# Linear attention and two mixing layers on one core: the decay table made by scans, first loads in halves, last product in two pieces

## The chip, the cores and the metric

The kernel runs on one core of one Trainium2 chip. Its engines are TensorE (matmuls, written PE in the profile; its weight loads are PEld), VectorE (DVE), ScalarE (ACT), GpSimd (POOL) and SyncE (SP), which issues most DMA transfers. Each engine works off its own list of instructions in order and waits on semaphores for the others. The metric is the device time of one execution in microseconds (us), the median of some runs.

## The reference

Three stages, batch 2, 768 tokens, 512 features. First an attention with a decaying state in 8 heads of 64 features:

```python
gamma = 1.0 - 2.0 ** (-5.0 - np.arange(H))
scale = 1.0 / np.sqrt(D)
for t in range(S):
    state = gamma[None, :, None, None] * state + np.einsum('bhd,bhe->bhde', k[:, :, t], v[:, :, t])
    y[:, :, t] = scale * np.einsum('bhd,bhde->bhe', q[:, :, t], state)
```

Then a token mixing of rank 32 and a layer of width 2048:

```python
u = x + ((x^T @ U) @ V)^T
x = u + np.maximum(u @ w_ch1, 0.0) @ w_ch2
```

And a gated layer with a spatial product:

```python
h = np.maximum(x @ w_in, 0.0);  u, v = h[..., :512], h[..., 512:]
v_n = (v - mean(v)) / sqrt(var(v) + 1e-6)
out = (u * (w_spatial @ v_n + b_spatial)) @ w_out
```

## The kernel before

The tokens stand in six chunks of 128. Attention is worked in eight *pairs* of heads, `i` = 0 to 7 (four for each batch), each with a `q`, `k` and `v` tile of 128 x 768 float32 (384 KB). For a pair, `scale` makes the decayed keys `kk` (for pairs 0 and 1 by transposing `k` on TensorE and scaling the six pieces on ACT or VectorE, for the others from a load), `scores` makes `sc` = k times q for each chunk in two halves of three chunks, and from it `pt`, scaled by `msc` and masked: on VectorE straight from PSUM (`L458`), or on ACT with a second product on POOL. The matmuls `ds` make each chunk's part of the state from `kk` and `v`, and a scan on VectorE (`L468`) sums them up with the decay into `s`. `mix` adds `pt` times `v` (the part within a chunk, `x<-pt`) and `s` times `q` (`x<-q`) in one bank and multiplies it by the table `gs`, which holds scale times gamma to the token's power, on VectorE (`L493`). The table is loaded into the first four planes of the tile `shared`; the fifth is the mask and the sixth the identity. `factors` spreads the decay for the scans over `decay` tiles by four copies on POOL (`L392`) from the tile `scales`, a small load that ACT issues.

After the pairs of a batch come transposes `t`, the products `g` (down) and `hu` (up) of the token mixing, and from then on large products of 128 x 384 in three passes (high parts, and the two mixed with a low part), which fill the rest: `c` and `acc` of the wide layer (some by seven products of half size instead of eight, `quad`), `qu` and `qv`, the spatial `pz`, and the last product `qo`. The last `quad`, `qo11`, ends with its product `3` into the bank `qo11d`; `final` adds a stored sum to it in two halves of 192 columns (`L884`) and stores them by two queues. Weights come in as 64-bit floats and are put together from integer words on ACT, VectorE and POOL (`L602` to `L607`).

The order of all this is made by a planner in the program (`Plan`). Every operation has a key, the engines on which it may run, and a cost in ns; `arrange` gives out operations in the order in which they can start, `settle` repeats that with keys shifted towards the latest start and keeps the best. A transfer ends by a rate and by delays from a table `DIPS`. Which engine runs an operation that has a choice is decided there too. `WARM` is the number of idle matmuls (`busy`) that TensorE runs while it waits for the first load. `LOADS` is the order of the loads: `h` is `k` in features by tokens, `q` and `v` are as named, `k` the loaded `kk`, `gs` the table.

Of the kernel before, what the change touches and what calls it, by code (L numbers as in the profile page):

```python
# [21 lines left out]
P = 128  # L22
# [21 lines left out]
class Plan:  # L44
# [48 lines left out]
    def arrange(self, sizes):  # L93
# [15 lines left out]
        dma, sent, sole = 0.0, 0, None  # L109
# [18 lines left out]
        def span(o, e, t0):  # L128
            st = max(free[e] - self.OVER[e], t0)
            for d in o.deps:  # L130
                if d.eng != "P" or e != "P":
                    st = max(st, d.end + self.LAG[d.eng] + (45.0 if e == "G" and d.eng != "G" else 0.0))
            if e == "P":
                st = max(st, free[e] + (0.0 if o.eng[e][1] == tiles else 130.0))
            elif o.eng[e][1] and port[1] not in (None, e):
                st = max(st, port[0] + (TIE if e == "G" else 0.0))
            return st, st + o.eng[e][0]
# [11 lines left out]
        while given < len(order):  # L149
            best, moved = None, False  # L150
            for e in self.ENGINES:
# [7 lines left out]
                low = min(c[3] for c in can) + SLACK.get(e, 30.0)  # L159
                for _, o, t0, st, en in sorted(can, key=lambda c: c[0]):  # L160
                    if st > low:
                        continue
# [48 lines left out]
    def latest(self):  # L211
# [4 lines left out]
        for o in sorted(self.ops, key=lambda o: (-o.start, -o.seq)):  # L216
# [7 lines left out]
            if e in "DE":  # L224
                t = min(t - 1500.0 - o.size / 210.0, free[e] - 430.0)
# [8 lines left out]
    def settle(self, sizes):  # L234
# [21 lines left out]
        if best is not now:  # L256
            go(best[1])
# [63 lines left out]
LOADS = "h0 q0 v0 h1 gs q1 v1 q2 h2 v2 k2 h3 k3 q3 v3 U V0 V1 w10 w11 q4 h4 k4 v4 w20 w21 q5 h5 v5 k5 q6 k6 k7 v6 q7 v7 h6 h7".split()  # L321
# [12 lines left out]
TURNED = (0, 1)  # L334
SEQ = [(m, b) for m in range(NM) for b in range(B)]
# [7 lines left out]
def tile_kernel(ctx: ExitStack, tc: tile.TileContext, a, out: bass.AP):  # L343
# [18 lines left out]
    NS = 2 * H + NP * (NCH - 1)  # L362
    sc_t = const.tile([P, NS + 1], F32, name="scales")
# [35 lines left out]
    def load(i, at):  # L399
# [35 lines left out]
    def scores(i):  # L435
# [25 lines left out]
        def run(_):  # L461
            for c in range(NCH - 1):
                for e in range(2):
                    r = slice(64 * e, 64 * e + 64)
                    mm(ds.t[r, :, c], kk_t[i].t[:, c, r], v_t[i].t[:, c, place(i, e)], True, True)
        op({"P": (625, "tokens")}, run, r=[(kk_t[i], 0), (kk_t[i], 1), v_t[i]], w=[ds])
# [3 lines left out]
    def mix(i):  # L470

        for h in range(2):
# [3 lines left out]
            for z, x in enumerate(xp):  # L476
# [5 lines left out]
                op({"P": (675, "tokens")}, intra, r=[v_t[i + z], (pt_t[i + z, 0], h), (pt_t[i + z, 1], h)], w=[x])  # L482
# [45 lines left out]
    def up(b):  # L528
        for h in range(2):
            for j in range(NP // 2):  # L530
# [6 lines left out]
                op({"P": (380, "up")}, run, r=[g_t[b], (vst, h)], w=u)  # L537
# [135 lines left out]
    def triple(o, start, stop, n, wh, wl, xh, xl, r, flip=False):  # L673

        def run(_):
            if flip:
# [7 lines left out]
        op({"P": pe(n, 3)}, run, r=r, w=[o])  # L684
# [43 lines left out]
    def rows(kind, m, gen, b):  # L728

        def product(o, pr, start):  # L730
            (wh, sh), (wl, sl) = W[kind, m][pr[0]]
            for k in range(2):
                x = F[gen, b, pr[1], k]
                h, l = (slice(z.start + k * P, z.start + (k + 1) * P) for z in (sh, sl))
                bh, bl = own(wh)[0], own(wl)[0]
                triple(o, start and k == 0, k == 1, T, lambda bh=bh, h=h: bh.t[:, h], lambda bl=bl, l=l: bl.t[:, l],
                       lambda x=x: x.t[:, 0, :], lambda x=x: x.t[:, 1, :], [wh, wl, (x, 0), (x, 1)])
# [138 lines left out]
    def final(b, m):  # L876
        ts = [Buf("a", [P, S], F32, f"out{b}{m}{z}") for z in range(2)]

        def store(i, h, src, add=None, y=None):
            t, d, cut = ts[i], 2 * m + i, slice(h * T, (h + 1) * T)  # L880
            if (b, m, i, h) == (B - 1, 1, 0, 1):
                for z, q in enumerate("ED"):
                    sl, to = slice(z * T // 2, (z + 1) * T // 2), slice(h * T + z * T // 2, h * T + (z + 1) * T // 2)
                    op({"V": vps(T // 2)}, lambda E, sl=sl, to=to: E.tensor_add(t.t[:, to], src.t[:, sl], add[0]()[:, sl]), r=[src, add[1]], w=[(t, h, z)])  # L884
                    dma(lambda to=to: out[b, d * P:(d + 1) * P, to], lambda to=to: t.t[:, to], P * T * 2, r=[(t, h, z)], eng=q)
# [9 lines left out]
        quad(f"o{b}{m}", T, rows("wo", m, 2, b), ys3(f"o{b}{m}"), store)  # L895
# [3 lines left out]
    with tc.manual_schedule():  # L899
        warm = nc.const_aps.tensor(1.0, (P, T), BF16)  # L900
        idle = bank([P, T], "idle")
# [20 lines left out]
        op({"A": (1500.0, False)}, lambda e: e.activation(sc_t[:, NS:NS + 1], warm[:, 0:1], AF.Copy))  # L922
# [93 lines left out]
def _arrays(q, k, v, moe_U, moe_V, moe_w_ch1, moe_w_ch2, moe2_w_in, moe2_w_spatial, moe2_b_spatial, moe2_w_out):  # L1016
# [13 lines left out]
    scale = 1.0 / np.sqrt(D)  # L1030
# [21 lines left out]
    def halves(x):  # L1052
# [4 lines left out]
        "gs": f32(gs.transpose(1, 0, 2)), "sc": f32(np.concatenate([ksc, msc, gc], axis=1)),  # L1057
# [26 lines left out]
```

## Time and profile before

| | |
|---|---|
| median of three runs | 451.77 us (451.09 to 451.88) |
| profiled execution | 451.47 us, span of its instructions 449.7 us |
| TensorE | 444.0 us busy, 99% of the span, 3232 matmuls |
| VectorE | 395.7 us, 88% |
| ScalarE | 241.6 us, 54% |
| GpSimd | 114.5 us, 25% |

The span runs from the first to the last instruction; what lies between it and the execution's time is start and end of the program. TensorE's share of 99% says that it is the engine that bounds the kernel, but the profile counts a matmul as busy from its start to its modelled end, so the share of a stretch must be read together with the waits. "Idle before" in square brackets names who ended a wait, by the semaphore that came last. The rows that matter stand below.

### The profile page before, as it was taken

What the parts mean: (1) busy time and instruction counts of PE and PEld (TensorE: products, weight loads), DVE (VectorE), ACT (ScalarE), POOL (GpSimd) and SP (SyncE); (2) the same over time, 40 slices, a digit from 0 to 9 for tenths busy, and PEclk for the clock granted to TensorE, in tenths of its full rate; (3) what the DMA queues carried; (4) which work ended last, traced back from release to release, by engine and by line L of the source; (5) the groups of instructions that cost most, each with busy time, mean ns of one, the idle gap of its engine ahead of it and who ended that gap; (6) DMA issues with size and microseconds to landing.
All of it is one profiled execution on the core that took longest, in us unless ns stands there. A gap on an engine that the chain in (4) does not pass through costs nothing.

```text
span 449.7 us, 8409 instructions
## 1 busy us (share of the span) xinstructions
PE 444.0 (99%) x3232; PEld 434.4 (97%) x3232; DVE 395.7 (88%) x843; ACT 241.6 (54%) x488; POOL 114.5 (25%) x117
## 2 busy tenths in 40 slices
PE   8999999999999999999999999999999999999996
PEld 6888799999999999999999999999999999999996
DVE  3779999999999899898897898999998999999943
ACT  3589686546456455645352444456757868353410
POOL 4378532434322121412031112111310002223000
PEclk9999999999999999999999999999999999999999
DMA  8998223022333232432232022000004210000033
GB/s 297 396 398 288 87 86 136 1 94 95 93 96 93 95 99 89 140 95 73 70 98 91 0 83 70 19 1 1 17 5 150 94 48 0 2 0 1 1 141 140
DMA packets 14151, 42.56 MB, mean 95 GB/s; under 512 B 1696, under 2 KB 2720, under 8 KB 14112
## 3 DMA queue, kind: packets, MB, share of 16 engines
q1 hardware_dynamic: 13824, 41.92, 27.1%
q8 instruction: 25, 0.41, 0.4%
q10 hardware_dynamic: 288, 0.12, 0.1%
q14 instruction: 14, 0.11, 0.1%
HBM read 38.88 MB, written 3.15 MB: 93 GB/s over the span
## 4 chain that ended last, share of the span: by engine, by line
PE 97%; DVE 1%; ACT 1%; issue 0%; DVEq 0%; ACTq 0%
PE acc L354 30%; PE pz L354 11%; PE c L354 4%; PE x L354 3%; PE sc L354 3%; PE ds L354 1%; PE t L509 1%; PE hu L354 1%; PE idle L354 1%; PE qu00c L354 0%; PE qu11d L354 0%; PE qo11d L354 0%; PE qu11c L354 0%; PE qu01a L354 0%; PE k L421 0%; PE qo11c L354 0%
## 5 line engine op out<-in xcount | busy, mean ns | idle before, releaser
L354 PE MATMUL acc<-a,hw 128*128 128x384 f32 x512 | 129.8, 334 | 0.0
L354 PEld LDWEIGHTS acc<-a,hw 128*128 128x128 f32 x512 | 92.5, 188 | 0.0
L354 PE MATMUL acc<-a,lw 128*128 128x384 f32 x256 | 85.5, 334 | 0.0
L795 DVE TENSOR_TENSOR x<-acc,x 128x384 f32<-128x384 f32 x128 | 69.3, 551 | 6.6 <-PE acc L354 6.0
L607 POOL TENSOR_TENSOR rw<-rw,tw 128x512 int32<-128x512 int32 x32 | 41.0, 1292 | 111.4 <-DVE rw L605 72.2
L354 PEld LDWEIGHTS acc<-a,lw 128*128 128x128 f32 x256 | 48.0, 188 | 0.0
L769 ACT ACTIVATE a<-y 128x384 fp32r<-128x384 f32 x42 | 22.0, 525 | 36.0 <-DVE y L763 34.3
L602 ACT ACTIVATE yw<-raww 128x512 f32<-128x512 f32 x32 | 21.3, 680 | 28.6 <-DVE rw L605 15.9
L770 DVE SCALAR_TENSOR_TENSOR a<-y,a 128x384 fp32r<-128x384 f32 x42 | 23.5, 559 | 0.9 <-ACT a L769 0.6
L605 DVE SCALAR_TENSOR_TENSOR rw<-yw,rw 128x512 uint32<-128x512 uint32 x32 | 23.4, 747 | 0.1
L603 ACT ACTIVATE tw<-raww 128x512 int32<-128x512 uint32 x32 | 21.4, 670 | 3.1 <-POOL rw L607 2.9
L456 POOL TENSOR_TENSOR pt<-pt,shared 128x384 f32<-128x384 f32 x16 | 15.7, 1005 | 14.9 <-ACT pt L455 12.9
L354 PE MATMUL pz<-ws,vn 128*128 128x384 f32 x108 | 19.0, 334 | 0.0
L354 PE MATMUL pz<-hws,vn 128*128 128x384 f32 x72 | 18.9, 334 | 0.0
L354 PEld LDWEIGHTS pz<-ws,vn 128*128 128x128 f32 x108 | 18.7, 188 | 0.0
L615 ACT CAST hw<-rw 128x512 fp32r<-128x512 f32 x18 | 11.2, 619 | 8.9 <-POOL rw L607 5.2
L616 DVE TENSOR_TENSOR lw<-rw,hw 128x512 fp32r<-128x512 f32 x18 | 12.7, 706 | 0.6 <-ACT hw L615 0.6
L855 POOL TENSOR_TENSOR ve<-r,ve 128x128 fp32r<-128x128 f32 x7 | 3.1, 461 | 39.0 <-DVE vn L855 20.1
L354 PEld LDWEIGHTS pz<-hws,vn 128*128 128x128 f32 x72 | 13.1, 188 | 0.0
L604 DVE TENSOR_SCALAR rw<-yw 128x512 uint32<-128x512 uint32 x32 | 13.0, 431 | 0.0
L354 PE MATMUL sc<-q,k 64*128 64x128 f32 x192 | 12.7, 280 | 0.0
L354 PEld LDWEIGHTS sc<-q,k 64*128 64x128 f32 x192 | 11.4, 189 | 1.3 <-issue 0.5
(1078 smaller groups left out, 1232.7 us busy)
## 6 DMA issues: line engine op xcount, KB each, us to landing
raww<-in_w SPq DMA_DIRECT2D x32, 512.0 KB, 3.6
k<-in_kT SPq DMA_DIRECT2D x8, 384.0 KB, 8.0
q<-in_qT SPq DMA_DIRECT2D x8, 384.0 KB, 7.9
v<-in_v SPq DMA_DIRECT2D x8, 384.0 KB, 8.1
kk<-in_k SPq DMA_DIRECT2D x6, 384.0 KB, 8.1
raws<-in_ws SPq DMA_DIRECT2D x6, 384.0 KB, 3.5
out_y<-out SPq DMA_DIRECT2D x6, 384.0 KB, 2.4
rawwu<-in_wu SPq DMA_DIRECT2D x4, 512.0 KB, 3.5
```

Of the source, the lines that this page charges most:

```text
L354: nc.tensor.matmul(o, l, r, start=start, stop=stop, skip_group_check=True)
L456: op({"G": gss(T)}, lambda E, pt=pt: E.tensor_mul(pt(), pt(), tri()), r=[(pt_t[i, e], h), TRI], w=[(pt_t[i, e], h)])
L602: op({"A": c}, lambda E: E.activation(y.t, words(1).bitcast(F32), AF.Copy, scale=2.0 ** -112), r=whole, w=[y])
L603: op({"A": c}, lambda E: E.activation(t.t, words(0), AF.Copy, scale=2.0 ** -29), r=whole, w=[t])
L604: op({"V": vone(n)}, lambda E: E.tensor_single_scalar(r.t, y.t.bitcast(U32), 3, ALU.logical_shift_left), r=[y], w=[r])
L605: op({"V": vss(n)}, lambda E: E.scalar_tensor_tensor(r.t, y.t.bitcast(U32), 0x80000000, r.t, ALU.bitwise_and, ALU.bitwise_or), r=[y, r], w ...
L607: op({"G": gss(n)}, lambda E: E.tensor_tensor(o().bitcast(I32), r.t.bitcast(I32), t.t, ALU.add), r=[r, t], w=[tok])
L615: op({"A": acp(DM)}, lambda E: E.copy(h.t, f(r.t)), r=[r], w=[h])
L616: op({"V": vss(DM), "G": gss(DM)}, lambda E: E.tensor_sub(l.t, f(r.t), f(h.t)), r=[r, h], w=[l])
L769: op({"A": (525, False)}, lambda E: E.activation(t.t[:, 0, :], y[0](), AF.Relu), r=[y[1]], w=[(t, 0)])
L770: op({"V": vss(T)}, lambda E: E.scalar_tensor_tensor(t.t[:, 1, :], y[0](), 0.0, f(t.t[:, 0, :]), ALU.max, ALU.subtract), r=[y[1], (t, 0)], ...
L795: op({"V": vps(T)}, lambda E, o=o, v=xs(b, d, h): E.tensor_add(v, o.t, v), r=[o, ("X", b, d, h)], w=[("X", b, d, h)])
```

## The change

The table `gs` is no longer loaded. Four scans on VectorE make it from the decay itself: plane `p` is a running product that begins at scale and multiplies by gamma at each column. So the powers begin at one instead of zero, and the host's `ksc` and `msc` are shifted by one to fit. The four gammas of a feature are four more columns of `scales`. The loads of `k`, `q` and `v` of pair 0 are each cut in two halves of three chunks (`h0 g0`, `q0 p0`, `v0 u0`), and `ds` of pair 0 has an operation for each half. The product `3` of the last `quad` is made in two pieces of 256 and 128 columns, each through all its six matmuls, and each added and stored by itself. The dummy activation at the start writes to another tile.

In the planner, matmuls before 5.2 us cost up to 1.9 times as much, loads have another rate and another table of delays, the rule by which TensorE picks its next operation is stricter, and after the search fifteen keys are moved by hand (`NUDGE`) and six operations fixed to an engine (`FIXED`).

```diff
@@ settings
-WARM = 9
+WARM = 7
-DIPS = {3: 450.0, 4: 450.0, 13: 900.0, 22: 300.0, 32: 300.0}
+DIPS = {15: 350.0, 22: 450.0, 32: 300.0}
+DIP, DIP0, DIP1 = 1100.0, 786e3, 1180e3
+COLD = 5200.0
-LOADS = "h0 q0 v0 h1 gs q1 v1 q2 h2 v2 k2 h3 k3 q3 v3 U V0 V1 ...
+LOADS = "h0 g0 q0 p0 v0 u0 h1 q1 v1 q2 h2 v2 k2 h3 k3 q3 v3 U V0 V1 ...
+CUT = (0,)
+CUTS = slice(0, 2 * P), slice(2 * P, T)
+NUDGE = {923: 2.36, 30: 0.93, 224: 4.13, ...
+FIXED = {365: 'G', 693: 'V', 156: 'V', 112: 'V', 69: 'V', 86: 'V'}
@@ load
-        dma(lambda: q_t[i].t[:], lambda: a["qT"][b, p], P * S * 4, w=[(q_t[i], 0), (q_t[i], 1)], key=at[f"q{i}"])
-        dma(lambda: k_t[i].t[:], lambda: a["kT"][b, p], P * S * 4, w=[(k_t[i], 0), (k_t[i], 1)], key=at[f"h{i}"])
+        for tile, src, names in ((q_t[i], "qT", "qp"), (k_t[i], "kT", "hg")):
+            for x, hs in zip(names, ((0,), (1,)) if i in CUT else ((0, 1),)):
+                cs = slice(hs[0] * T, (hs[-1] + 1) * T)
+                dma(lambda tile=tile, cs=cs: tile.t[:, cs], ...
-        if i == 0:
-            dma(lambda: shared.t[:, 0:NP, :], lambda: a["gs"], NP * P * P * 4, w=GS, key=at["gs"])
@@ rows
-            for k in range(2):
+            for cut in cuts if pr == PRODUCTS["3"] and cuts else (None,):
+                for k in range(2):
@@ final
-                for z, q in enumerate("ED"):
-                    sl, to = slice(z * T // 2, (z + 1) * T // 2), slice(h * T + z * T // 2, h * T + (z + 1) * T // 2)
+                for sl, q in zip(CUTS, "ED"):
+                    n, to = sl.stop - sl.start, slice(h * T + sl.start, h * T + sl.stop)
@@ start of the program
+        ones = nc.const_aps.tensor(1.0, (P, P), F32)
             factors(p)
+            plan.key = AT0
+            op({"V": (440, False)}, lambda E, p=p: E.tensor_tensor_scan(gs(p), sc_t[:, NS - NP + p:NS - NP + p + 1].to_broadcast([P, P]), ones, D ** -0.5, ALU.mult, ALU.mult), r=["sc"], w=[GS[p]])
@@ host
-    ksc = gamma[None, :] ** (P - t[:, None])
-    msc = gamma[None, :] ** -t[:, None]
+    gm = heads(np.repeat(gamma, D), 0).reshape(NP, P).T
+    ksc = gamma[None, :] ** (P - 1 - t[:, None])
+    msc = gamma[None, :] ** (-1 - t[:, None])
```

How this moves the instructions is seen at three places. The first is the head of VectorE's list, the first thing it does in the program: `kk` is scaled from the transposed `k`, `pt` made from `sc`, `s` is the scan over `ds`. Before:

```order
L426 TENSOR_SCALAR kk_146<-k_133,scales 128x3x64
L426 TENSOR_SCALAR kk_146<-k_140,scales 128x3x64
L458 SCALAR_TENSOR_TENSOR pt_173<-sc_153,scales,shared 128x384
L458 SCALAR_TENSOR_TENSOR pt_177<-sc_154,scales,shared 128x384
L468 SCALAR_TENSOR_TENSOR s_204<-decay_118,ds_179 128x320
```

The same head of VectorE's list in the change:

```order
L952 SCALAR_TENSOR_TENSOR shared<-scales,const-float32-1.0 128x128 x4
L447 TENSOR_SCALAR kk_141<-k_128,scales 128x3x64
L447 TENSOR_SCALAR kk_141<-k_135,scales 128x3x64 x2
L479 SCALAR_TENSOR_TENSOR pt_170<-sc_146,scales,shared 128x384
L479 SCALAR_TENSOR_TENSOR pt_174<-sc_147,scales,shared 128x384
L492 SCALAR_TENSOR_TENSOR s_201<-decay_116,ds_178 128x320
```

The four scans (`shared<-scales`) stand first, and VectorE has three of the four scalings of `kk` instead of two.

The second place is TensorE's list behind pair 0's first `x` products, where pair 1 begins: `k` are the transposes, `sc` the scores, `x_230` the second half of pair 0's `x` products. Before:

```order
L421 MATMUL k_210<-shared,k_120 128x128 x3
L421 MATMUL k_215<-shared,k_120 128x128 x3
L354 LDWEIGHTS const-bfloat16-1.0
L354 MATMUL x_230<-const-bfloat16-1.0 128x384
L354 MATMUL x_230<-pt_173,v_116 64x128
L354 MATMUL x_230<-pt_177,v_116 64x128
...
L354 MATMUL sc_242<-q_126,k_120 128x128
L354 MATMUL sc_243<-q_126,k_120 128x128
```

TensorE at the same place in the change, where `x_269` is that second half and `x_280` belongs to pair 1:

```order
L442 MATMUL k_207<-shared,k_133 128x128 x3
L442 MATMUL k_214<-shared,k_133 128x128 x3
L373 MATMUL sc_223<-q_139,k_133 128x128
L373 MATMUL sc_224<-q_139,k_133 128x128
...
L373 MATMUL ds_251<-v_144,kk_218 64x64 x10
L373 MATMUL x_269<-pt_170,v_122 64x128
L373 MATMUL x_269<-pt_174,v_122 64x128
...
L373 MATMUL x_280<-pt_247,v_144 64x128
```

The second half of pair 0's `x` products moved from ahead of pair 1's `sc` to behind its `ds`, and the idle matmul in front of it is gone.

The third place is the end of TensorE's list, the product `3` of the last `quad`. Before:

```order
L354 MATMUL qo11c<-f21t_5327,qwo_5057 128x384 x3
L354 MATMUL qo11d<-f21b_5255,hsbwo_5118 128x384 x2
L354 MATMUL qo11d<-f21b_5255,lsbwo_5132 128x384
L354 MATMUL qo11d<-f21b_5293,hsbwo_5118 128x384 x2
L354 MATMUL qo11d<-f21b_5293,lsbwo_5132 128x384
```

The end of TensorE's list in the change:

```order
L373 MATMUL qo11c<-f21t_5330,qwo_5059 128x384 x3
L373 MATMUL qo11d<-f21b_5258,hsbwo_5124 128x256 x2
L373 MATMUL qo11d<-f21b_5258,lsbwo_5135 128x256
L373 MATMUL qo11d<-f21b_5296,hsbwo_5124 128x256 x2
L373 MATMUL qo11d<-f21b_5296,lsbwo_5135 128x256
L373 MATMUL qo11d<-f21b_5258,hsbwo_5124 128x128 x2
L373 MATMUL qo11d<-f21b_5258,lsbwo_5135 128x128
L373 MATMUL qo11d<-f21b_5296,hsbwo_5124 128x128 x2
L373 MATMUL qo11d<-f21b_5296,lsbwo_5135 128x128
```

Six matmuls of 384 columns became six of 256 and, behind them, six of 128.

## Rows read from the trace of the kernel before

**Rows 1.** Busy us in stretches: PE, PEld, DVE, ACT, POOL, then clock, DMA share, GB/s:

```profile
7.71:53.18 45.47, 45.41 (x847) 39.58 (x848) 36.86 (x69) 31.71 (x66) 27.53 (x28) 1.00 0.81 306
55.77:446.22 390.45, 390.45 (x2331) 390.05 (x2328) 354.23 (x765) 204.97 (x414) 83.18 (x78) 1.00 0.20 66
```

**Rows 2.** Waits of PE in the whole execution: us in total, times, longest:

```profile
PE hu L354 <- ACT gt L496: 0.7, 1, 0.7
PE ds L354 <- DVE pt L458: 0.6, 1, 0.6
```

**Rows 3.** Timeline of PE, first 12 us: start us, us, instructions, idle before:

```profile
0.84 3.04 PE L354 MATMUL idle<-const-bfloat16-1.0 128*128 128x384 bf16 x9 [0.84 <-PEq L1073]
...
4.00 1.49 PE L421 MATMUL k<-shared,k 128*128 128x128 f32 x6
5.41 1.70 PE L354 MATMUL sc<-q,k 64*128 64x128 f32 x24
7.71 0.80 PE L354 MATMUL ds<-v,kk 128*64 128x64 f32 x20 [0.60 <-DVE pt L458]
8.32 0.86 PE L354 MATMUL x<-pt,v 128*64 128x128 f32 x12
9.11 0.87 PE L421 MATMUL k<-shared,k 128*128 128x128 f32 x6
...
10.88 1.61 PE L354 MATMUL sc<-q,k 64*128 64x128 f32 x24
```

**Rows 4.** Timeline of DMA issues, first 11 us: start us, us, queue, transfer:

```profile
0.80 0.41 ACTq L360 DMA_DIRECT2D scales<-in_sc  x1
1.70 0.42 SPq L360 DMA_DIRECT2D v<-in_v  x1
...
9.23 0.33 SPq L360 DMA_DIRECT2D kk<-in_k  x1
10.21 0.33 SPq L360 DMA_DIRECT2D q<-in_qT  x1
```

**Rows 5.** From issue to landing: `scales` (issued 0.80), then `v` (1.70):

```profile
DMA to landing us min/median/max: 3.2/3.2/3.2
...
DMA to landing us min/median/max: 5.9/5.9/5.9
```

**Rows 6.** Timeline of DVE, 5 to 8 us:

```profile
5.34 0.42 DVE L426 TENSOR_SCALAR kk<-k,scales 128x192 f32<-128x192 f32 x1 [5.34 <-ACT kk L426]
...
6.56 1.14 DVE L458 SCALAR_TENSOR_TENSOR pt<-sc,scales,shared 128x384 f32<-128x384 f32 x2 [0.17 <-PE sc L354]
```

**Rows 7.** Timeline of POOL, 4 to 6 us:

```profile
4.09 1.64 POOL L392 COPY decay<-scales 128x320 f32<-128x320 f32 x4 [2.36 <-DMA scales<-in_sc]
```

**Rows 8.** DVE beside POOL: a scan, an `L605`, and all its `rw` (ns min/median/max):

```profile
33.73 1.96 POOL L456 TENSOR_TENSOR pt<-pt,shared 128x384 f32<-128x384 f32 x2
34.00 0.82 DVE L468 TENSOR_TENSOR_SCAN s<-decay,ds 128x320 f32<-128x320 f32 x1 [1.36 <-PE ds L354]
...
271.79 1.29 POOL L607 TENSOR_TENSOR rwv<-rwv,twv 128x512 int32<-128x512 int32 x1 [9.05 <-DVE rwv L604]
272.03 1.60 DVE L605 SCALAR_TENSOR_TENSOR rwv<-ywv,rwv 128x512 uint32<-128x512 uint32 x1
...
L605 DVE SCALAR_TENSOR_TENSOR rw<-yw,rw x32: 677/682/1607, 47.8 to 225.2; 128x512 uint32<-128x512 uint32 x32
```

**Rows 9.** Chain of waits, both `hu`: start us, us, what:

```profile
33.95 1.83 PE hu L354 x15
...
54.21 1.57 PE hu L354 x16
```

**Rows 10.** Timeline of the last matmuls and adds:

```profile
445.01 0.51 PE L354 MATMUL qo11d<-f21b,hsbwo 128*128 128x384 f32 x2
...
445.88 0.34 PE L354 MATMUL qo11d<-f21b,lsbwo 128*128 128x384 f32 x1
446.26 0.62 DVE L884 TENSOR_TENSOR out<-qo11d,yo 128x192 f32<-128x192 f32 x2 [0.49 <-PE qo11d L354]
```

More of the change, by code (lines that the diff above doesn't have):

```diff
@@ L136, in span @@
                 st = max(st, port[0] + (TIE if e == "G" else 0.0))
-            return st, st + o.eng[e][0]
+            cost = o.eng[e][0]
+            return st, st + cost + (min(max(0.0, COLD - st), 1.9 * cost) * 0.9 / 1.9 if e == "P" and cost < 2000.0 else 0.0)
         def harm(o, x):
@@ L159, in arrange @@
                 low = min(c[3] for c in can) + SLACK.get(e, 30.0)
+                if e == "P":
+                    low = min(c[3] + (SWITCH if c[1].eng[e][1] != tiles else 0.0) for c in can)
                 for _, o, t0, st, en in sorted(can, key=lambda c: c[0]):
-                    if st > low:
+                    if st + (SWITCH if e == "P" and o.eng[e][1] != tiles else 0.0) > low:
                         continue
@@ L224, in latest @@
             if e in "DE":
-                t = min(t - 1500.0 - o.size / 210.0, free[e] - 430.0)
+                t = min(t - 1500.0 - o.size / 250.0, free[e] - 430.0)
             else:
@@ L255, in settle @@
             best = min(best, now)
-        if best is not now:
-            go(best[1])
+        self.base = best[1]
+        keys = list(best[1])
+        for k, d in NUDGE.items():
+            keys[k] += d
+        for k, e in FIXED.items():
+            start[k] = {e: start[k][e]}
+        self.go, self.choices = go, start
+        go(keys)
     def give_out(self, engines, pools, idle, tie):
@@ L459, in scores, with run @@
         ds = bank([P, D, NCH - 1], f"ds{i}")
[L461 to L466, printed above, removed]
+        for hs in ((0,), (1,)) if i in CUT else ((0, 1),):
+            cs = range(hs[0] * TC, min(NCH - 1, (hs[-1] + 1) * TC))
+            def run(_, cs=cs):
+                for c in cs:
+                    for e in range(2):
+                        r = slice(64 * e, 64 * e + 64)
+                        mm(ds.t[r, :, c], kk_t[i].t[:, c, r], v_t[i].t[:, c, place(i, e)], True, True)
+            op({"P": (125 * len(cs), "tokens")}, run, r=[(kk_t[i], 0), (kk_t[i], 1)] + [(v_t[i], h) for h in hs], w=[ds])
         s_t[i] = s = Buf("s", [P, D * (NCH - 1)], F32, f"s{i}")
@@ L726, in own, with rows @@
         return x if isinstance(x, tuple) else (x, None)
-    def rows(kind, m, gen, b):
+    def rows(kind, m, gen, b, cuts=()):
         def product(o, pr, start):
             (wh, sh), (wl, sl) = W[kind, m][pr[0]]
-            for k in range(2):
[L733 to L737, printed above, removed]
+            for cut in cuts if pr == PRODUCTS["3"] and cuts else (None,):
+                for k in range(2):
+                    x = F[gen, b, pr[1], k]
+                    h, l = (slice(z.start + k * P, z.start + (k + 1) * P) for z in (sh, sl))
+                    bh, bl = own(wh)[0], own(wl)[0]
+                    triple(o, start and k == 0, k == 1, T if cut is None else cut.stop - cut.start, lambda bh=bh, h=h: bh.t[:, h], lambda bl=bl, l=l: bl.t[:, l],
+                           lambda x=x: x.t[:, 0, :], lambda x=x: x.t[:, 1, :], [wh, wl, (x, 0), (x, 1)] + [(o, c.start) for c in cuts if cut is not None and c.start < cut.start], cut=cut)
         return product
```

46 lines of the change are left out of this document (28 added, 18 removed).

## Prediction

> **What bounds the kernel now.** I read the stretches first, then TensorE's waits, then the timeline of the first 14 us and of the end. Between 55.77 and 446.22 us TensorE is busy for 390.45 of 390.45 us [rows 1]: no edit that leaves its matmuls alone can shorten that stretch, only a new wait can lengthen it. The change can gain in two places, the 55.77 us ahead and the 3.5 us behind. Ahead, TensorE shows two waits worth naming, 0.7 us before the `hu` products and 0.6 us before the first `ds` [rows 2]; from 7.71 to 53.18 it is busy for 45.41 of 45.47 us [rows 1]. The start goes like this [rows 3]: idle matmuls to about 4.0, six transposes of `k`, 24 `sc` matmuls from 5.41, a hole, `ds` at 7.71. The profile puts the hole down to VectorE's `pt`, but `v` was issued at 1.70 and took 5.9 us [rows 4, 5]: it landed at 7.6, just ahead of 7.71. So `v` and `pt` (6.56 + 1.14 = 7.70 [rows 6]) ended together. After that the loads come one per 0.98 us (SyncE's issues at 9.23 and 10.21, each held back until an earlier load has landed [rows 4]).
>
> **Times and baseline.** The profiled execution took 451.47 us (span 449.7, 1.8 around it), 0.30 below the median of 451.77. I form the sum against 451.47 and add 0.30.
>
> **The change, part by part.** *Loads.* The table's 256 KB go: at 384 KB per 0.98 us [rows 4], 0.65 us for everything behind `h1`. Pair 0 in halves adds three issues of about 0.42 each [rows 4], which runs beside the transfers. The first `k` half lands earlier by at most half of its 384 KB, 0.5 us, and TensorE begins near 3.5 instead of 4.0. That alone buys nothing: the next thing that is late is `v`, and behind it VectorE.
>
> *Four scans.* They stand first in VectorE's queue, ahead of `kk` and `pt` of pair 0; in before VectorE was free until 5.34 [rows 6]. One scan of 320 elements takes 0.82 [rows 8]; for 128 I take 0.42 (bounds 0.33, in proportion, and 0.82), 1.47 for four, overlapped by 0.07 each. But they start on the landing of `scales`, and so do POOL's four `decay` copies, 1.64 us from 4.09 [rows 7]. Here the trace has two kinds of row. A scan that reads one operand from PSUM ran its 0.82 beside a POOL product that began at 33.73. `L605`, which reads two tiles in SBUF, takes 0.68 as a rule and 1.60 when it meets POOL's `L607`, and ends 0.55 after POOL does [rows 8]. The new scan reads `scales` and the constant 1.0, both in SBUF, so I place it with `L605`: scans and copies take turns. I take 2.9 for the four scans: 1.47 and three to four copies of 0.41 (2.7 to 3.1).
> The Trainium skill says the same in "SBUF — State Buffer", "Who interferes with whom": a VectorE instruction with two SBUF inputs contends with a GpSimd instruction that reads SBUF, and the loser waits for the whole instruction. The `L605` rows agree; no row here has a scan of that kind. Without the rule the scans would end about 1.4 us earlier (first rival).
>
> *VectorE's chain.* `scales` landed at 4.0 (0.80 + 3.2 [rows 4, 5]). With half the bytes of `k` beside it I take a start of 3.75 (3.4 to 4.1). Then 2.9 for the scans, 1.1 for three `kk` (one more than in before; 0.42 each [rows 6]) and 1.14 for two `pt`: 8.89 (8.3 to 9.4). In before it was 7.70. So a wait on `pt` takes the place of the wait on `v`: the first `x` products start at 8.95, not at 8.32 [rows 3]. Queued behind those `pt` are the scan `s_201` and the `kk` of pair 1, which TensorE needs only after the next `sc`.
>
> *TensorE's order.* In before the other six `x` products of pair 0 (`x_230`) and an idle matmul stood between pair 1's transposes and its `sc`; now they stand behind its `ds`. Pair 1's `sc` thus starts at 8.95 + 0.79 (`x`, 8.32 to 9.11) + 0.80 (`k`; 0.87 with the drain) = 10.54, against 10.88 [rows 3]. Its `q` has landed by then: in before `k`, table and `q` followed `v` (7.6 + 0.98 + 0.65 + 0.98 = 10.2), now without the table. From 10.88 before needed 42.30 us to 53.18. The changed order adds the moved `x`, 0.67 (0.79 less an array change of about 0.12), and has two changes of the array's division fewer, 0.2. The first `hu` took 1.83 against 1.57 for the second [rows 9]; six `x` products now stand in front of it and cover `gt`: 0.26 less. Smaller waits that show as long groups I put at 0.15 less (0 to 0.3). 42.30 + 0.67 - 0.2 - 0.26 - 0.15 = 42.36, so the stage ends at 52.90 instead of 53.18: -0.28 (-0.8 to +0.5 over the bounds of the chain). The `gt` copy and its 0.7 us wait stay: ACT has the same three instructions ahead of it in both orders.
>
> *End.* The last six matmuls of 384 columns start 0.174 apart, 445.01 to 445.88; two adds of 192 columns end at 446.88 [rows 10]. Now six of 256 columns (two thirds, 0.12 apart) and six of 128. For the latter no row has this form: in proportion 0.06, and the transposes with 128 columns stand at 0.87 / 6 = 0.145 at most [rows 3]. I take 0.12, nearer to the transposes. The last then starts 0.4 later (0.1 to 0.55), and behind it comes one add of about 0.28 instead of two that end 0.62 after the first begins. That is even within 0.2 either way; with 64 KB to store instead of 96 I take -0.05.
> The Trainium skill ("TensorE: Matmul & The Clock Gate", "LDWEIGHTS (loading the stationary operand)") prices a weight load by its columns, 107 ns for 128; by that the pieces of 128 stand at 0.107 and the end gains 0.1 instead of 0.05.
>
> *The rest.* Four idle matmuls fewer, the dummy activation's new target and the planner's edits cost nothing of their own: they act through the order, counted above. In the stretch of 390 us I take 0.
>
> Sum: -0.28 - 0.05 = -0.33: 451.14 in the profiled execution, **451.4** as a median.
>
> **Rivals.** *A, the scans do not wait for POOL.* For it: the scan rows at 34.00 [rows 8]. Against it: that one reads PSUM. Then `pt` ends at 3.75 + 1.47 + 1.1 + 1.14 = 7.46 and the loads decide. If the second half of `v` lands at 7.6 as before, `q` of pair 1 follows two loads later, 7.6 + 1.96 + 0.13 = 9.7; if the late `v` was an accident, it lands at 6.3 (`q` plus one step of 0.98) and `x` starts at 7.5, `sc` at 9.1. The stage ends 52.06 or 51.46, gain 1.1 to 1.7, and with the end 450.0 to 450.6: **450.3**.
>
> *B, slower: TensorE's clock falls in the new hole.* Between the `sc` of pair 0 (now over near 6.5) and 8.95 TensorE has only `ds`. In before six transposes took 1.49 at 4.00 and 0.87 at 9.11 [rows 3], the lower level against the upper (1.2 and 2.4 GHz), though the clock column reads 1.00 in each stretch [rows 1]. If the clock falls there and needs the 4.6 us again that it took from 0.84 to 5.41, half of these are lost: +2.3, **453.7**. It decides as soon as the hole is long enough to drop the clock; the 0.6 and 0.7 us of [rows 2] were not, this one is about 2.
>
> *C, slower: one wait in the 390 us.* All its margins were met before, the whole list is rearranged, and each meeting of `L605` with POOL costs 0.9 [rows 8]. Two such in front of a product that TensorE has reached give 451.4 + 1.8 = **453.2**; one alone would stay near 452.3.
>
> **How the numbers follow.** Forecast 0.54, A 0.31, B 0.05, C 0.10. A measurement of this kernel tells 0.2% (0.9 us) from no change, so faster is below 450.87 and slower above 452.67. Faster: 0.26 from A and 0.10 from the forecast's lower end, 0.36. Slower: B, 0.07 of C and 0.02 of the upper end, 0.14. Same: 0.50. The range leaves out B, most of C and the best of A: 450.0 to 452.5. The forecast's own range is 450.8 to 452.2.
>
> **What would show it.** In the changed profile: four scans whose mean is near 0.8 rather than 0.42, ending near 6.6; a wait of TensorE on `pt` before the first `x`, which starts near 8.95; pair 1's `sc` near 10.5; the stage's last wait at `hu` unchanged at 0.7; 390 us without a wait; the last matmul later by 0.4 and the last add ending within 0.2 of 446.88, both counted from the end of the matmul stage. Scans of 0.42 back to back and `x` right behind `ds` would mean A. Transposes of pair 1 spaced as those of pair 0 would mean B.

## The result and the profile after

The changed kernel is slower: 454.54 us (454.03 to 454.87, 4 runs) against 451.54 (451.09 to 451.88, 4 runs), a ratio of 1.0070 with an interval of 1.0058 to 1.0082. The prediction was 451.4 in a range of 450.0 to 452.5. The profiled execution took 454.03, its span is 452.3; before they were 451.47 and 449.7.

The same places as in [rows 1], cut where the same work begins: to the first `sc` of pair 1, to the first `c`, to the first of the last product's matmuls, to the end (columns as in [rows 1]).

```profile
0.00:9.94 9.94, 8.56 (x76) 6.15 (x76) 4.91 (x10) 3.39 (x6) 4.84 (x13) 1.00 0.75 248
9.94:56.42 46.48, 44.92 (x826) 38.31 (x826) 39.02 (x75) 31.04 (x64) 25.89 (x27) 1.00 0.78 293
56.42:446.85 390.43, 389.64 (x2324) 389.13 (x2323) 352.50 (x761) 205.64 (x417) 88.48 (x81) 1.00 0.20 65
446.85:452.30 5.45, 1.49 (x13) 1.35 (x12) 1.18 (x3) 0.00 (x0) 0.00 (x0) 0.85 0.40 144
```

And the kernel before, cut at the same work:

```profile
0.00:10.88 10.88, 9.43 (x92) 6.55 (x92) 3.54 (x7) 4.13 (x8) 4.65 (x13) 1.00 0.83 294
10.88:55.77 44.89, 44.14 (x815) 37.83 (x814) 37.34 (x71) 32.46 (x67) 26.66 (x27) 1.00 0.78 293
55.77:445.01 389.24, 389.24 (x2325) 389.16 (x2323) 353.67 (x764) 204.97 (x414) 83.18 (x78) 1.00 0.20 65
445.01:449.70 4.69, 1.21 (x7) 0.89 (x6) 1.18 (x3) 0.00 (x0) 0.00 (x0) 0.96 0.47 168
```

The differences are -0.94, +1.59, +1.19 and +0.76, together 2.6. In this execution the start gains what was wished for and more; all three later stretches lose. The start differs from one execution to the next by more than its gain, as the ledger below shows. TensorE's longest waits, against [rows 2] (us in all, count, longest):

```profile
PE idle L373 <- PEq L1104: 0.8, 1, 0.8
PE ds L373 <- DVE x L517: 0.8, 1, 0.8
PE qu10a L373 <- ACT yu L520: 0.8, 1, 0.8
PE hu L373 <- ACT gt L520: 0.7, 1, 0.7
```

The `hu` wait is as it was, the first `ds` wait is gone, a `ds` of pair 2 and a `qu10a` in the 390 us wait anew. The groups answering to [rows 3] and [rows 9]:

```profile
3.47 1.51 PE L442 MATMUL k<-shared,k 128*128 128x128 f32 x6 [0.23 <-DMA k<-in_kT]
5.16 2.43 PE L373 MATMUL sc<-q,k 64*128 64x128 f32 x24 [0.18 <-DMA q<-in_qT]
7.52 0.80 PE L373 MATMUL ds<-v,kk 128*64 128x64 f32 x20
8.15 0.85 PE L373 MATMUL x<-pt,v 128*64 128x128 f32 x12
...
9.94 1.61 PE L373 MATMUL sc<-q,k 64*128 64x128 f32 x24
...
15.71 1.43 PE L373 MATMUL x<-q,s 64*64 64x128 f32 x40
17.99 0.80 PE L373 MATMUL ds<-v,kk 128*64 128x64 f32 x20 [0.84 <-DVE x L517]
...
33.93 0.83 PE L373 MATMUL x<-pt,v 128*64 128x128 f32 x12
34.69 2.46 PE L373 MATMUL hu<-vst,gt 32*128 32x384 f32 x16
37.09 1.09 PE L373 MATMUL x<-pt,v 128*64 128x128 f32 x16
```

VectorE and GpSimd at the start, against [rows 6] and [rows 7]: the four scans take 1.99 and the copies beside them 2.21, and `pt` waits 0.45 for `sc`, not for the scans.

```profile
3.54 1.99 DVE L952 TENSOR_TENSOR_SCAN shared<-scales,const-float32-1.0 128x128 f32<-128x128 f32 x4 [3.54 <-DMA scales<-in_sc]
3.57 2.21 POOL L411 COPY decay<-scales 128x320 f32<-128x320 f32 x4 [1.85 <-DMA scales<-in_sc]
5.46 1.04 DVE L447 TENSOR_SCALAR kk<-k,scales 128x192 f32<-128x192 f32 x3
6.94 1.14 DVE L479 SCALAR_TENSOR_TENSOR pt<-sc,scales,shared 128x384 f32<-128x384 f32 x2 [0.45 <-PE sc L373]
```

And the end, against [rows 10]: both adds start after the last of the twelve matmuls (448.07 to 448.34), the first one too.

```profile
447.44 0.28 PE L373 MATMUL qo11d<-f21b,lsbwo 128*128 128x256 f32 x1
...
448.07 0.28 PE L373 MATMUL qo11d<-f21b,lsbwo 128*128 128x128 f32 x1
448.38 0.62 DVE L913 TENSOR_TENSOR out<-qo11d,yo 128x256 f32<-128x256 f32 x2 [0.77 <-PE qo11d L373]
```

### The profile page after: what moved, and what is told of

It reads as the page before. It is cut to its first block, busy times and chain, and to the rows that moved or that the text cites. A ratio compares the mean times of both kernels' runs of the same rounds, so it can differ in the third digit from the quotient of the medians.

```text
span 452.3 us, 8426 instructions
## 1 busy us (share of the span) xinstructions
PE 444.6 (98%) x3234; PEld 434.9 (96%) x3234; DVE 397.6 (88%) x848; ACT 240.1 (53%) x485; POOL 119.2 (26%) x119
## 4 chain that ended last, share of the span: by engine, by line
PE 91%; DVE 3%; ACT 1%; POOL 1%; issue 0%; DVEq 0%; POOLq 0%; ACTq 0%
PE acc L373 28%; PE pz L373 11%; PE c L373 4%; PE x L373 3%; PE sc L373 2%; PE t L533 1%; PE ds L373 1%; PE hu L373 1%; DVE s10t L587 1%; PE qo11d L373 1%; DVE x L824 1%; PE qo00c L373 0%; PE q71c L373 0%; PE qu11c L373 0%; PE qo11c L373 0%; PE qo11a L373 0%
## 5 line engine op out<-in xcount | busy, mean ns | idle before, releaser
L629 DVE SCALAR_TENSOR_TENSOR rw<-yw,rw 128x512 uint32<-128x512 uint32 x32 | 22.3, 715 | 0.0
L631 POOL TENSOR_TENSOR rwv<-rwv,twv 128x512 int32<-128x512 int32 x4 | 5.2, 1290 | 38.0 <-DVE a L799 20.6
L373 PE MATMUL sc<-q,k 64*128 64x128 f32 x192 | 13.7, 292 | 0.3 <-DMA q<-in_qT 0.2
```

What stands on the lines that cost most here:

```text
L373: nc.tensor.matmul(o, l, r, start=start, stop=stop, skip_group_check=True)
L629: op({"V": vss(n)}, lambda E: E.scalar_tensor_tensor(r.t, y.t.bitcast(U32), 0x80000000, r.t, ALU.bitwise_and, ALU.bitwise_or), r=[y, r], w ...
L631: op({"G": gss(n)}, lambda E: E.tensor_tensor(o().bitcast(I32), r.t.bitcast(I32), t.t, ALU.add), r=[r, t], w=[tok])
```

## Experiments

Each row of the table is the time against the kernel before, run on the same chip. Single steps of 0.3 to 0.8 us lie near what these intervals tell apart, so the verdicts rest on the stretches of the profiles; the times are the cross-check.

| kernel | us | before | ratio |
|---|---|---|---|
| changed kernel | 454.54 | 451.54 | 1.0070 (1.0058 to 1.0082) |
| e1 last product whole | 454.03 | 451.29 | 1.0060 (1.0042 to 1.0078) |
| e2 `s10t` on VectorE | 454.21 | 451.29 | 1.0059 (1.0043 to 1.0074) |
| e3 idle in thirds | 454.63 | 451.29 | 1.0066 (1.0041 to 1.0091) |
| e4 copies behind scans | 454.40 | 451.29 | 1.0066 (1.0046 to 1.0086) |
| e5 `acc` ahead of `qu10a` | 453.73 | 451.31 | 1.0057 (1.0042 to 1.0072) |
| e6 `hu` first | 454.01 | 451.31 | 1.0063 (1.0048 to 1.0078) |
| e7 pair 0 whole | 454.68 | 451.31 | 1.0077 (1.0062 to 1.0092) |
| e8 before with scans | 451.17 | 451.31 | 1.0000 (0.9991 to 1.0010) |
| e9 nine idle matmuls | 454.23 | 451.52 | 1.0062 (1.0048 to 1.0076) |
| e10 four steps undone | 452.81 | 451.52 | 1.0032 (1.0019 to 1.0044) |
| e11 e8 and `gt` ahead | 451.10 | 451.52 | 0.9988 (0.9979 to 0.9997) |
| e12 before, nine memsets | 451.99 | 451.52 | 1.0009 (1.0000 to 1.0018) |

All kernels in the changed order keep each engine's list as planned; only what is named is moved in it. The edits are shortened to the lines that matter, and those of e4, e7 and e12 are partly put in words. The kernel before itself differs by up to 0.25 us between the chips (451.29 to 451.54), so small differences between rows of different chips say little.

**e1: the last product whole.**

```diff
-CUTS = slice(0, 2 * P), slice(2 * P, T)
+CUTS = slice(0, T // 2), slice(T // 2, T)
-rows("wo", m, 2, b, CUTS if (b, m) == (B - 1, 1) else ())
+rows("wo", m, 2, b, ())
```

Both adds then name the whole bank as what they read, as in before.

> The changed kernel with the last product in one piece of 384 columns and two adds of 192, as in before; nothing else moves. Theory: in the changed kernel both last adds started at 448.38, 0.04 after the end of the last of the twelve matmuls (448.34), so cutting the product let no add start early and only cost matmul time: from the start of the last product to the end of the last add it took 2.15 us there and 1.86 in before. Expected here: 1.86 again, and the time 0.3 lower than the changed kernel's 454.5, 454.2. Rival: what stands behind the last add (0.4 us more in the closing instructions than in before) belongs to the cut too; then 0.7 lower, 453.8. If the cut is harmless, the same 454.5.

Its timeline of the end:

```profile
446.95 0.51 PE L373 MATMUL qo11d<-f21b,hsbwo 128*128 128x384 f32 x2
...
447.82 0.34 PE L373 MATMUL qo11d<-f21b,lsbwo 128*128 128x384 f32 x1
448.19 0.62 DVE L913 TENSOR_TENSOR out<-qo11d,yo 128x192 f32<-128x192 f32 x2 [0.49 <-PE qo11d L373]
```

From the product's start to the end of the adds: 446.95 to 448.81, 1.87, against 2.15 in the changed kernel and 1.86 in before. The cut costs 0.29. The program's closing instructions, from the landing of the last store to the end, still took 1.52, as in the changed kernel; the rival falls.

**e2 and e5: the wait in the 390 us.** First `s10t` was moved from GpSimd to VectorE; then, after that had failed, products were put in front of the waiting one (and VectorE's last operation for them, `a<-y,a`, ahead of two `s10t`).

```diff
+        self.ops[1584].eng = "V"                                   # e2: s10t
...
+        self.ops[1533].start = self.ops[1575].start + 1.0          # e5: a<-y,a ahead of two s10t
+        # e5: three groups of acc products right ahead of op 1691, qu10a
```

> The changed kernel with one subtraction (s10t, 384 columns, two tiles in SBUF, started by GpSimd at 306.11 in the changed kernel's trace) done by VectorE at the same place of its queue. Theory: the only wait in the 390 us (TensorE idle 309.07 to 310.20, 0.95 lost) comes from GpSimd and VectorE meeting: s10t took 1.34 there and VectorE's next two-tile operation 1.37 instead of 0.55; ScalarE's casts and the yu copy stand behind that. Without GpSimd there, the wait falls to under 0.2 and the time by 0.8 to 0.95, to 453.6 to 453.7. Rival: ScalarE's own queue sets the yu copy; then the wait stays at 0.8 and the time at 454.5.

> The changed kernel with three groups of acc products (9 matmuls, 1.56 us) moved ahead of the qu10a product that waits in the 390 us, and with VectorE's last operation for them (a<-y,a) moved ahead of two s10t. Theory (formed after the run with s10t on VectorE left that wait at 0.95): nothing meets there; qu10a must begin again in its bank as soon as ScalarE's yu copy has read it, and yu stands behind two casts. In before a qu10d product of 3 matmuls stood in between, in the changed kernel nothing. With 1.56 us of other products in front the wait goes: 0 to 0.2 left, time 0.8 to 1.0 below the changed kernel's 454.5, 453.5 to 453.7. Rival: what waits is the f10t operand chain on VectorE, late as a whole; then the hole moves behind the acc products and the time stays at 454.5.

In e2 nothing met any more, and the wait stayed, 0.8 in the same row: the theory falls, its rival holds. ScalarE's timeline of the changed kernel shows why, with that of before below it:

```profile
308.46 0.49 ACT L836 ACTIVATE x<-qu00a 128x384 f32<-128x384 f32 x1
308.85 0.91 ACT L592 CAST f10t<-s10t 128x384 fp32r<-128x384 f32 x2
309.67 0.48 ACT L520 COPY yu<-qu10a 128x384 f32<-128x384 f32 x1
```

```profile
307.82 0.49 ACT L807 ACTIVATE x<-qu00a 128x384 f32<-128x384 f32 x1
308.28 0.48 ACT L496 COPY yu<-qu10a 128x384 f32<-128x384 f32 x1
```

`qu10a` may begin again in its bank (of PSUM, where TensorE writes) only when `yu` has read it. In before `yu` came right behind `x<-qu00a`, and a `qu10d` product stood between; in the changed order two casts stand ahead of `yu`, and TensorE's next product is `qu10a` itself. With 1.56 us of `acc` in between (e5) the row is gone from the longest waits:

```profile
PE idle L373 <- PEq L1104: 0.8, 1, 0.8
PE hu L373 <- ACT gt L520: 0.7, 1, 0.7
PE sc L373 <- DMA q<-in_qT: 0.7, 1, 0.7
```

From the first `c` to the last product it then takes 389.67 instead of 390.43. The median is 0.8 lower (0.6 by the ratios), with intervals that overlap. The last 0.4 over before are small holes, one of 0.24 before a later `qu00c`. That `yu` stands behind two casts was not undone by itself; shown is that other products in front of the waiting one cover its wait.

**e3: the hole in front of `ds` of pair 2.** In the changed profile TensorE's weight load shows it as `issue`, time in which it waited for nothing that the profile shows, although the waits' list names an `x` of VectorE:

```profile
17.96 0.25 PEld L373 LDWEIGHTS ds<-v,kk 128*64 128x64 f32 x5 [1.00 <-issue]
```

```diff
-mm(idle, warm[:, 0:P], warm)                     # 7 times 384 columns
+mm(idle.t[:, 0:P], warm[:, 0:P], warm[:, 0:P])   # 21 times 128 columns
```

> The changed kernel with its 7 idle matmuls of 384 columns at the start written as 21 of 128 columns: the same columns and the same end of the idle work near 3.1, but 28 more instructions in TensorE's queue ahead of everything else. In the changed kernel TensorE stood still from 16.87 to 17.77 us in front of the ds products of pair 2, although every semaphore that they wait for had been reached by 15.85. Theory: TensorE ran out of instructions; its next 16 KB of code were moved at 15.18 to 16.25, behind the loads. Then the hole of about 0.9 us moves 28 instructions ahead, into the middle of the 40 x products of q and s, where nothing is waited for, and ds follows x at once; the time stays within 0.3 of 454.5. Rival: the hole belongs to what ds waits for (data, a bank of PSUM); then it stays in front of ds, at 0.8 to 0.9.

No hole came at all: `ds` followed `x` at once, at 17.55, and within 0.1 us so it did in every other run. The packet of 16 KB of instructions went at 14.20 to 15.28 there, against 15.18 to 16.25. So the theory was not tested. That `ds` does not need the `x` that the waits' list names is seen in e4, where it started at 17.64, before that `x` had ended (17.38 to 18.39). For the theory speaks e4 again, the next latest: its packet ended at 15.98, and `ds` came 0.09 late, TensorE going on 1.48 after the packet's end; in the changed profile 1.52. That the hole is a late code load is argued, not shown; that the changed order does not bring it every time is shown, since it came in one profile of ten in that order.

**e4: the copies behind the scans.**

```diff
+        for k in (4, 6, 8, 10): self.ops[k].start = self.ops[11].start + 0.01 * k
+        tie(self.ops[4].ins, self.ops[11].ins)       # first copy waits for the last scan
```

> The changed kernel with GpSimd's four decay copies held until VectorE's four scans are done. In the changed kernel the scans ran from 3.54 to 5.53, 1.99 in all, beside the copies (0.58 to 0.64 each instead of 0.45). Theory: the two take turns; alone, the four scans take 1.4 to 1.5 (pitch 0.34 to 0.36 instead of 0.52) and the copies 0.45 each. The time does not follow: the first pt waited 0.45 for sc, so the chain had that much to spare; expected 454.5 within 0.2. Rival: the scans are that slow by themselves (pitch 0.52, total 1.99 again).

VectorE's and GpSimd's rows:

```profile
3.58 1.37 DVE L952 TENSOR_TENSOR_SCAN shared<-scales,const-float32-1.0 128x128 f32<-128x128 f32 x4 [3.58 <-DMA scales<-in_sc]
```

```profile
5.01 1.64 POOL L411 COPY decay<-scales 128x320 f32<-128x320 f32 x4 [3.28 <-DVE shared L952]
```

Alone, 1.37 and 1.64; together 1.99 and 2.21. Scans and copies do hinder each other. The time stayed the same, as expected.

**e6: `hu` ahead of the `x` products.**

```diff
+        self.ops[197].start = self.ops[198].start - 1.0      # x of pair 4, first half, behind hu
```

The edit also keeps the planner from putting an idle matmul into the gap that it opens (31 to 36 us).

> The changed kernel with the first half of pair 4's x products (12 matmuls) put back behind the first hu products, as in before. In the changed kernel the 16 hu took 2.39 us, in before 1.83. Theory: the x products in front hold a bank of PSUM, so the last two hu banks wait for VectorE's adds; with x behind, hu takes 1.8 again and the matmul stage ends 0.5 earlier, the time 0.3 to 0.6 below 454.5 (454.0). Rival: VectorE's adds start no earlier, whichever comes first; then hu takes 2.4 in either order, and the time is the same within 0.2.

```profile
34.65 1.90 PE L373 MATMUL hu<-vst,gt 32*128 32x384 f32 x16
36.48 1.75 PE L373 MATMUL x<-pt,v 128*64 128x128 f32 x28
```

`hu` takes 1.83 to the next start instead of 2.39, and from the `sc` of pair 1 to `c` it is 44.99 instead of 45.57 to 45.69 (the runs without the hole). The `x` group in front of `hu` costs 0.57 there; the median is 0.5 lower (0.3 by the ratios), with intervals that overlap. That it costs so much by holding a bank is argued from the changed profile, where the last two weight loads of `hu` wait 0.6 for VectorE's adds, which empty the banks of the first `hu`:

```profile
36.25 0.29 PEld L373 LDWEIGHTS hu<-vst,gt 32*128 32x128 f32 x2 [0.60 <-DVE x L564]
```

**e7 and e8: the loads.** In e7 pair 0 is loaded whole again; e8 is before, with nothing but the scans in place of the table.

```diff
-dma(k, q, v of pair 0, first half); dma(..., second half)
+dma(k, q, v of pair 0, whole)                                   # e7
...
-dma(lambda: shared.t[:, 0:NP, :], lambda: a["gs"], ...)
+[nc.vector.tensor_tensor_scan(gs(x), gm[x], ones, D ** -0.5, mult, mult) for x in range(NP)]   # e8
```

> The changed kernel with k, q and v of pair 0 loaded whole (three loads of 384 KB in place of six of 192), each engine's order unchanged. In four of the five profiles with halves the k of pair 1 landed at 8.82 to 9.46 (in before 8.55) and its q at 9.8 to 10.4 (before 10.20 with the table's 256 KB ahead of it). Theory: the halves cost what the table's load saves. Whole, k of pair 1 lands near 8.6 and its q near 9.6; TensorE begins at 3.9 instead of 3.4, the sc of pair 1 start near 9.8 instead of 9.9 to 11.2, and the time falls by 0.3 to 0.7, to 453.8 to 454.2. Rival: the gap in the loads near 7 to 8.5 us comes at the same time either way; then q lands at 9.8 to 10.4 and the time stays at 454.5 within 0.2.

> The kernel before, in its own order, with only the table of the decay made by the four scans on VectorE (first in its queue) in place of its load: no halves, the old planner, the old last product. Theory: the scans themselves cost nothing and gain nothing, since in before the sc of pair 1 wait for the x products in front of them (10.07 to 10.88) and not for q (10.20): the same as before, 451.3 within 0.3; all of the 3 us come from the order that was made anew, and from the tail. Rival A: the freed 0.65 us of loading is worth something: 450.7. Rival B: the scans and the copies on GpSimd hold up kk and pt (scans until 6.0, pt until 8.1 instead of 7.7): 451.7 to 452.

The loads did what the theory said. With whole loads and no table (e7, e8, e11) the `q` of pair 1 landed at 8.58, 8.97 and 8.83; with halves and no table (nine profiles) at 9.80 to 10.42. The halves cost the load stream 0.8 to 1.8 us. With whole loads and the table that `q` landed at 10.20 (before) and 9.46 (e12), so the halves took back what the table's removal had given. The time of e7 did not fall; in its profile TensorE was late by itself, on `sc` and `ds`, with `q` long there:

```profile
5.50 2.93 PE L373 MATMUL sc<-q,k 64*128 64x128 f32 x24
8.37 1.33 PE L373 MATMUL ds<-v,kk 128*64 128x64 f32 x20
```

e8 is the same as before, within 0.1%: neither the scans nor the freed load move the time. In its profile, too, `ds` waits for `v` (0.65).

**e9: nine idle matmuls.** In most profiles the 24 `sc` of pair 0 had one of two durations; in some they changed from the longer to the shorter on the way. First e7, then e4 (ns, least, median, most):

```profile
L373 PE MATMUL sc<-q,k x24: 417/417/580, 5.5 to 8.0; 64*128 64x128 f32 x24
```

```profile
L373 PE MATMUL sc<-q,k x24: 272/272/373, 5.5 to 6.9; 64*128 64x128 f32 x24
```

Their starts are spaced 1.9 times as far (2.86 against 1.54 in all), the lower of TensorE's two levels (1.2 and 2.4 GHz) against the upper, though the granted clock reads 1.00 in both.

```diff
-op({"P": (n * 320.0, False)}, lambda _: spend(n), w=[idle])
+op({"P": (n * 320.0, False)}, lambda _: spend(n + 2), w=[idle])
```

> The changed kernel with 9 idle matmuls at the start instead of 7, so that they run until the transposes of k, as in before. In five of seven profiles with 7 of them TensorE stayed on its lower level until about 10 us: the first 24 sc took 2.86 us instead of 1.54 and the first ds 1.12 instead of 0.63, and the sc of pair 1 started at 11.0 to 11.5; where the level rose by 5.2 they started at 9.9 to 10.4. In both profiles with 9 idle matmuls (before, and before with scans) the level had risen by 5.4. Theory: the stillness between idle matmuls, k and sc (0.2 to 1.1 us) is what holds the level down. With 9, the first sc take 1.54 (plus a wait for q), the sc of pair 1 start by 10.5, and the time falls by 0.3 to 1.0, to 453.5 to 454.2. Rival: the level rises late by chance; then half of it remains, sc takes 2.86 again, and the time stays at 454.5.

```profile
5.51 2.17 PE L373 MATMUL sc<-q,k 64*128 64x128 f32 x24 [0.35 <-DMA q<-in_qT]
7.61 0.80 PE L373 MATMUL ds<-v,kk 128*64 128x64 f32 x20
```

The level rose within the first `sc`, and the `sc` of pair 1 started at 10.15. Over all profiles: with seven idle matmuls' worth of work at the start five of eight were still on the lower level in `ds` at 8.3 to 9.7, with nine none of six. But four of those six are in before's order, and with seven the level rose early in three, so that the idle work decides the level is likely, not shown. The time is 0.3 lower, which the intervals do not tell from nothing; what the idle work is worth stays open.

**e10: four steps undone together** (the edits of e1, e5, e6 and e9).

> The changed kernel with four steps together: 9 idle matmuls, hu ahead of the x products, acc products ahead of qu10a, last product whole. Scans and halves stay. Theory: the losses add, each being a hole in a TensorE that is otherwise busy: 0.3 to 1.0 (start), 0.57 (hu), 0.75 (the wait in the 390 us), 0.29 (tail) from 454.5: 451.9 to 452.6; what is left over before is 0.4 us in the closing instructions and 0.4 in small holes. Rival: loads or VectorE's queue take up part of it; then 453 or more.

452.81, 1.7 below the changed kernel and 0.2 to 0.9 short of the sum. In the profile the single gains are there: 1.83 for `hu`, 389.67 to the last product, 1.87 at the end. What falls short is the stage: the `sc` of pair 1 began at 10.15, but from there to `c` it took 45.95 instead of 44.99. TensorE lost 0.37 inside the `ds` of pair 2, whose `kk` had landed at 16.46 (14.83 in e6), 0.33 in front of a later `sc` and 0.28 among `x` products:

```profile
17.28 1.17 PE L373 MATMUL ds<-v,kk 128*64 128x64 f32 x20
```

That is no price of the early start as such: e9 began at the same 10.15 and took 45.59, like the kernels that began late (45.57).

**e11: before with the scans, and `gt` one place earlier.**

```diff
+        self.ops[289].start = self.ops[250].start + 1.0      # e8, and one tw behind gt on ScalarE
```

> The kernel before with scans in place of the table's load, and in ScalarE's queue the second gt copy ahead of one conversion (tw) that takes 0.66 us. In before the only wait of TensorE behind the start, 0.7 us ahead of the second hu, ends with that copy. Theory: gt starts 0.4 to 0.5 us earlier, hu and the 390 us follow, 450.8 (0.4 below before). Rival: what comes later on ScalarE or GpSimd (the conversion is needed for weights) gives it back: 451.2, the same.

The one wait that both kernels kept, against [rows 9]:

```profile
51.71 1.52 PE L354 MATMUL g<-xtok,ust 128*32 128x128 f32 x48
53.16 0.34 PE L354 MATMUL hu<-const-bfloat16-1.0 128*128 128x384 bf16 x1
53.67 1.57 PE L354 MATMUL hu<-vst,gt 32*128 32x384 f32 x16 [0.17 <-ACT gt L496]
```

The wait falls from 0.7 to 0.2, and the 390 us follow unchanged (389.24). 451.10 against 451.52: 0.12% faster than before, with an interval (0.03 to 0.21%) that just leaves out no change.

**e12: what ends the program.** From the last landing to the end before takes 1.06, the changed kernel 1.52, and so did the others in its order (1.39 to 1.52).

```diff
-e.memset(shared.t[:, NP:NP + 2, :], 1.0)                       # 256 columns
+nine memsets of 16 to 32 columns                               # 8 instructions more on GpSimd
```

> The kernel before with GpSimd's first memset (256 columns) written as nine, that is 8 instructions more on GpSimd, as many as the changed kernel has more there (201 records against 193). From the landing of the last store to the end of the span before takes 1.06 us, before with scans 1.00, every kernel in the changed order 1.39 to 1.52, with GpSimd's DRAIN near the end 0.3 to 0.4 us late. Theory: GpSimd's code is loaded in pieces (8 KB each in the records of the DMA engines), and with 8 instructions more the end of a piece falls into the closing instructions; the stretch then takes 1.4 to 1.5 here too, and the time rises by 0.4, to 451.7. Rival: the closing depends on something else (DMA queues, engines' order); then 1.0 to 1.1 and 451.3.

The closing took 1.50, and the median rose by 0.47 (by the interval of the ratio 0.0 to 0.8). GpSimd's closing rows, here and then in before (ns, least, median, most):

```profile
L1080 POOLq DRAIN  x3: 34/225/3944, 404.4 to 449.5; - x3
```

```profile
L1080 POOLq DRAIN  x3: 34/78/3931, 404.7 to 449.4; - x3
```

The changed kernel has the same 225. The traces show more than the run was made for. In all eleven profiles with 200 to 202 GpSimd records (its queue's waits and drains counted), that engine stands still for 0.32 to 0.38 us in front of its 197th record, whichever instruction that is: this `DRAIN` where there are 201 records, the instruction behind it in e2 (200), the one ahead of it in e4 (202). The three profiles with 193 records have no such gap among their closing instructions. So 0.45 of the loss in the closing goes with a place in GpSimd's list that its 193 records do not reach. That a new piece of code begins at that place is argued.

## Why the prediction was wrong

Ledger of the 2.6 us between the two profiles, term by term: start -0.94; hole before `ds` of pair 2 +0.9; `hu` +0.57; the rest of the stage +0.1; wait at `qu10a` +0.95; small holes in the 390 us +0.2; last product and adds +0.29; landing +0.07; closing +0.45. The hole belongs to that execution, and so does the start's gain. In the other seven profiles with seven idle matmuls' work the `sc` of pair 1 began 0.5 to 1.5 later, at 10.41 to 11.47; over all eight the mean is 10.91. In the four profiles in before's order (before, e8, e11, e12) it began at 10.42 to 10.96, on average at 10.67. So over the runs the changed start gained nothing, and the -0.94 was luck.

- *Loads.* The first half of `k` did land 0.5 earlier (3.33). The term "0.65 us for everything behind `h1`" failed: three more issues were counted as free beside the transfers, and `q` of pair 1 landed at 9.8 to 10.4, where whole loads with the table had it at 10.20 and 9.46 (e7, e8, e12).
- *Scans.* That scans and copies take turns was right, the size was not: 1.99, not 2.9. Alone four scans take 1.37 and four copies 1.64 (e4); together 2.2, not 3.0. The Trainium skill ("SBUF — State Buffer", "Who interferes with whom") calls the port pair that VectorE and GpSimd share an exclusive lock. With a wait for the whole instruction the two would have taken 3.0; here each of the eight instructions became longer by some 0.15 us (0.62 and 0.57 over four), less than half of its 0.34 and 0.41. The rival without turns was no nearer: `pt` waited for `sc`.
- *VectorE's chain.* "the first `x` products start at 8.95": 8.15, with `sc` and not the scans in front of `pt`. Over the runs it was 7.5 to 9.7, late where TensorE's level was the lower one. Rival B had that mechanism and the wrong place: the level did not fall in a later hole, it rose late.
- *Stage.* "0.26 less" for `hu` was the step with the wrong sign: +0.57 (e6). The moved `x`, 0.67, was right (0.66). Without the hole the stage took 45.57 to `c`, where 42.36 + 1.03 + 1.56 = 44.95 had been forecast (to the end of `g`, then the idle matmul and the second `hu` as in before). Of the 0.62 missed, `hu` alone makes 0.83 (a gain of 0.26 that became a loss of 0.57); the other terms together came out 0.2 better than forecast.
- *The 390 us.* "In the stretch of 390 us I take 0" failed, and it is the largest single step: +1.19, of which 0.95 at one wait. Rival C had the event, one wait, and the wrong cause: no meeting of VectorE and GpSimd (e2), but TensorE's order with nothing between two uses of one bank (e5). Both lists of that place, TensorE's and ScalarE's, were there to be compared before the run.
- *End.* The pieces of 128 columns were near their price of 0.12, 0.10 to 0.12 apart. "one add of about 0.28 instead of two" failed: the first add waited for the last piece. In the trace only the last of the twelve matmuls updates the semaphore that the first add waits for, so the stretch cost 0.29 more than in before instead of 0.05 less (e1).
- *Not in the sum at all*: 0.45 in the closing instructions, put at nothing without a reason (e12).

The forecast of "same" and the chance of 0.14 for slower came from treating every stretch without a wait as safe. Behind the start each loss of TensorE's order (`hu`, `qu10a`, the last adds) is read here as a buffer that is read or handed over later than before, at a place that showed no wait of that kind.

## What to carry to other kernels

Where one engine is busy without a gap, an edit that makes the schedule anew is to be priced by the places where its list now differs, each with the buffer that it reuses and who reads that buffer last; a gain at the start is one term among them. A piece of work cut in two helps its reader only if the first piece signals by itself. Before halving a first load, look whether the load stream itself, and not only its first landing, becomes later.

## What was not expected of the hardware

- Eight more instructions on GpSimd, all at the start, lengthened the end of the program by 0.43 us (1.06 to 1.50) and the median by 0.47. In every profile with 200 or more GpSimd records that engine stood still for 0.32 to 0.38 us in front of the 197th.
- TensorE stood 0.9 us with no wait that the profile shows, after a 16 KB packet of instructions had gone between loads of pair 2 and 3, 15.18 to 16.25. The Trainium skill ("Runtime: NRT & Kernel Launch", "Instruction fetch mechanics") says that code is streamed in blocks of 16 KiB and that crossing a boundary is mostly hidden. The 25 packets of 16 KB in the page's queue list agree with the size; beside loads that fill the queues the crossing may not have been hidden, here in one execution.
- Six loads of 192 KB in place of three of 384 KB made the load behind the next one land at 9.8 to 10.4 instead of 8.6 to 9.0, with the same bytes.
- The same 24 matmuls took 1.54 us in one profile (e4) and 2.86 in another (e7), with the same list for TensorE and a granted clock that reads 1.00.
